# Attention and a two-layer network on one core: the second group's first product as seven half-size products, with a new instruction order

## The chip, the cores and the metric

The kernel runs on one core of a Trainium2 chip. A core has five engines with queues of their own: PE multiplies matrices (weights are loaded by rows called PEld), DVE, ACT and POOL work elementwise, SP issues DMAs here (ACT issues a few at the end). PE writes to PSUM only, POOL does not use PSUM in this kernel. The metric is the device time of one execution in microseconds (us); lower is better.

## The reference, cut to what matters

```
q, k, v: (8 batches, 8 heads, 576 rows, 64)
phi(x) = concat(relu(x) * cos(theta), relu(x) * sin(theta))      theta = pi/2 * row / 576
kv  = phi(k)^T v          z = sum over rows of phi(k)
x   = (phi(q) kv) / (phi(q) z + 1e-6)         -> (4608 tokens, 512)
h   = x @ w_in            (512 x 2048)
g   = max(0.01 h, h)
out = g @ w_out           (2048 x 512)
```

Inputs and output are float32; the kernel's products take float16 and add in float32.

## The kernel before, in words

The tokens are worked in nine groups of 512: groups 0 to 7 are the first 512 rows of each batch, group 8 the last 64 rows of all eight batches. For each group the kernel goes through these steps, whose names are used below (`g` is the group):

- `Lq`, `Lk`, `Lv`, `Lw1`, `Lw2` (for groups 0 and 1 and the weights) and `lq`, `lk`, `lv` (later groups) load; `cw` and `w` cast the weights w_in (w1) and w_out (w2) to float16.
- `rq`, `rk` take the relu, `kt` multiplies k by the angles, `q` prepares phi(q), `v` casts v, `kv` sums phi(k)^T v, `ko` copies it out.
- `qT` transposes phi(q) by a DMA, `n` multiplies it by kv, `N` divides (three DVE instructions), `xT` transposes x by a DMA. In groups 0 and 1 the transposes are made on PE (`qt`, `xt`) and copied out (`qo`, `xo`).
- `f` is the first product (x @ w_in), `F` the second (g @ w_out), `O` takes a result out of PSUM and `D` stores it.

The first product of a group takes 64 matmuls of 512 columns in the plain form (`ffn1`, 16 blocks of 128 outputs by four chunks of the 512 inputs), and eight ACT instructions `e` that apply the leaky relu to two blocks each. In the other form (`ffn1s`) the product is cut in quarters and computed by Strassen's scheme in Winograd's variant: seven products of half the size in place of eight. There are four units `u` in a group, and in each seven products `f{g}.{u}.1` to `.7` of four matmuls of 256 columns. Sums of quarters go in and come out: `W` are sums of w1's quarters (eight in all, made once), `X` four sums of x's quarters for each group. A unit has three of the four PSUM banks `ps_f`, and nine elementwise steps: `b`, `s`, `u` copy a bank (DVE or ACT, as the order says), `y`, `z` add on DVE, `a`, `c`, `e`, `d` apply the leaky relu on ACT. The second product takes the same scheme for all groups but group 0 (`G7 = 1`): sums `T` of w2, sums `S` of g, seven products `F{g}.{n}`, sums `M` and `O`. In the kernel before, the first product takes it from group 2 on (`F7 = 2`).

The order of all instructions is written out in the string ORDER, one token for each step. Each engine runs its own instructions in that order; SP's and ACT's DMAs too. `:D`, `:A`, `:P` after a token name the engine (DVE, ACT, POOL), and `@n` the place in a ring of buffers (of staged loads, of PSUM banks or of outputs) that the step's tile takes. A step waits for its inputs, and for the earlier readers of its place. `i` are idle matmuls at the start. The tokens of different groups are interleaved: while the first and second products of one group run on PE, the elementwise work and the transposes of the next are done.

Where the stage of w1's second block lies in `wext`, `Lk1.0` later takes that room, and the sums `W` of w1 take it after that.

Of the kernel before, what the change touches and what calls it, by code (L numbers as in the profile page):

```python
# [37 lines left out]
xo0.1.0:A f0.1.c f0.2.c f0.3.a f0.1.b f0.3.c N0.1.1 cw.2:P cw.3:P xo0.0.1:D Lw1.5 f0.0.b xt0.1.1@0
f0.0.d f0.2.d f0.3.d f0.0.c Lw1.7 Lw1.8 xo0.1.1:D f0.3.e f0.4.a f0.0.e f0.2.e e0.1 cw.4:D f0.4.d
f0.1.d f0.1.e cw.8:D cw.5:D f0.5.a f0.5.d Lw1.6 Lq1@3 rq1.1:D rq1.0:D cw.7:P e0.0 f0.6.a@0 f0.6.d  # L40
f0.7.a q1.3.0:D q1.1.1:D f0.7.d Lw2.0@2 e0.2 q1.0.0:D q1.2.1:D q1.0.1:D q1.2.0:D w0.0:D Lk1.0 w0.2:D
cw.6:P e0.3 Lw2.1@1 q1.3.1:P f0.12@1 w1.0:P f0.13 rk1.0:D W1.1:D W0.1:D f0.14@0 f0.15 kt1.0.0 e0.6
# [1 line left out]
qt1.2@1 F0.2.2 F0.1.0@1 F0.0.2 qt1.0@0 qo1.2:D qt1.1@1 w1.2:A Lv1.0 Lk1.1 v1.0:P qo1.0:D qo1.1:D
kt1.0.1 F0.0.4 F0.1.2 F0.0.6 F0.3.4 F0.3.6 kv1.0@1 F0.1.4 rk1.1:A kt1.1.0 F0.1.6 Lw2.2@0 Lw2.3.0
w2.0:D ko1.0:A n1.1.0@1 F0.2.4 F0.2.6 kt1.1.1 w2.2:A w3.0:A N1.1.0 F0.2.8 F0.3.8 n1.0.0@0 N1.0.0
F0.0.8 F0.3.10 F0.3.12 Lw2.3.2 w3.2:D F0.0.10 F0.2.10 F0.2.12 xt1.0.0@0 F0.2.14 Lv1.1 v1.1:A kv1.1@1
ko1.1:A lq2@3 rq2.0:P rq2.1:A F0.3.14 T1 q2.0.1:P q2.3.0:P O0.2:D@0 lk2@1 lv2.0@2 F0.0.12 n1.0.1@1
q2.2.1:P F0.0.14 O0.0:A@3 O0.3:D@1 n1.1.1 F0.1.8 F0.1.10 N1.0.1 xt1.1.0@1 xt1.0.1@0 F0.1.12 N1.1.1
# [6 lines left out]
F1.1.1.0 S1.1a S1.1b F1.1.1.1 F1.2.0.1 q3.2.0:D S1.1c F1.1.0.1 S1.2a F1.2.1.1 v3.0:A q3.1.0:A
q3.3.1:P q3.0.1:P q3.2.1:P v3.1:A kv3 M1.1:A S1.2b S1.2c F1.6.0.0@0 F1.6.1.0 F1.6.1.1 q3.3.0:A
q3.1.1:D S1.3c F1.6.0.1 O1.2@2 F1.5.0.0@1 xT2 S1.3a W0.3:D X2.1:D f2.0.1 S1.4b X2.2:D X2.3:D
F1.5.0.1 F1.5.1.0 f2.0.5 q3.0.0:A rq4.0:A ko3:A b2.0:A s2.0:A f2.0.6 M1.6 X2.4:P S1.3b f2.0.2 f2.1.1
D0.2 qT3.1 qT3.0 u2.0:D f2.0.3 F1.7.0.0 f2.0.7 rq4.1:A a2.0 z2.0 e2.0 F1.7.1.0 F1.7.1.1 f2.1.5 y2.0  # L60
b2.1:A S1.4a q4.0.0:A s2.1:A q4.1.0:D lv4.0@2 lv4.1 lk4@3 q4.2.1:P f2.0.4 c2.0 F1.5.1.1 n3.0 f2.1.6
D0.3 D1.2 q4.3.0:P q4.0.1:P D0.0 u2.1:A q4.1.1:A d2.0 f2.1.2 W1.2:P F1.7.0.1 f2.1.3 a2.1 W1.4:P
W1.3:P N3.0 lq5@0 f2.1.7 n3.1 f2.2.1 v4.1:P rk4.0:P M1.7 z2.1 F1.4.1.0 F1.4.0.0 rk4.1:P y2.1 f2.2.5
f2.1.4 e2.1 b2.2:A c2.1 f2.2.2 s2.2:A N3.1 n3.2 f2.2.6 q4.3.1:A d2.1 u2.2:A O1.5@0 v4.0:A f2.2.3
F1.3.1.0 F1.3.1.1 f2.2.7 N3.2 z2.2 n3.3 f2.3.1 F1.4.1.1 F1.4.0.1 F1.3.0.0 N3.3 y2.2 O1.4@1 e2.2
kt4.0.0 kt4.0.1 kt4.1.0 b2.3:A q4.2.0:A F1.3.0.1 f2.3.6 F2.1.0.0@0 a2.2 f2.3.5 u2.3:A c2.2 s2.3:A
f2.3.7 f2.2.4 F2.1.1.0 d2.2 f2.3.2 f2.3.3 y2.3 c2.3 a2.3 xT3 kt4.1.1 S2.1a z2.3 O1.3@2 qT4.0 X3.1:P
X3.2:P f2.3.4 d2.3 e2.3 kv4 f3.0.1 b3.0:A f3.0.5 F2.1.0.1 F2.1.1.1 f3.0.6 X3.3:D S2.1b S2.3b f3.0.2
M2.1:A ko4:A s3.0:D F2.2.0.0 f3.0.3 f3.1.1 n4.0 u3.0:A f3.0.7 F2.2.0.1 F2.2.1.0 F2.2.1.1 a3.0 S2.2a
S2.1c S2.3c S2.2c z3.0 e3.0 F2.6.0.0@1 b3.1:A rq5.1:A F2.6.1.0 f3.1.6 f3.1.2 N4.0 O2.2:D@3 S2.2b  # L70
y3.0 n4.1 u3.1:A lk5@2 rk5.0:P F2.6.1.1 f3.1.5 rq5.0:P q5.0.1:P q5.0.0:A X3.4:P qT4.1 D1.3 lv5.0@1
c3.0 rk5.1:A s3.1:A F2.5.0.0@0 f3.1.7 F2.5.1.0 F2.6.0.1 f3.0.4 N4.1 kt5.0.0 f3.1.3 D1.5 D2.2 lq6@3
q5.1.1:P v5.0:P q5.1.0:P d3.0 a3.1 lv5.1 F2.5.1.1 kt5.0.1 y3.1 z3.1 M2.6 n4.2 f3.2.1 F2.5.0.1 f3.1.4
f3.2.5 S2.3a e3.1 b3.2:A N4.2 kt5.1.0 kt5.1.1 f3.2.6 u3.2:A f3.2.2 F2.7.1.0 qT5.0 D1.4 f3.2.7 c3.1
a3.2 n4.3 F2.7.1.1 s3.2:A N4.3 d3.1 y3.2 f3.3.5 F2.7.0.0 F2.7.0.1 M2.7 f3.2.3 z3.2 O2.5@0 S2.4a
f3.3.1 S2.4b rq6.1:A s3.3:A q5.2.1:A c3.2 e3.2 v5.1:P q5.2.0:D S3.1a f3.2.4 S3.3a F2.4.0.0 b3.3:A
q5.3.1:D f3.3.3 kv5 F2.4.1.0 ko5:A d3.2 xT4 f3.3.6 F2.4.0.1 f3.3.2 n5.0 F2.4.1.1 rq6.0:P q5.3.0:P
u3.3:A f3.3.7 z3.3 X4.1:D S3.2a f4.0.1 F2.3.0.0 F2.3.0.1 y3.3 q6.1.0:P X4.2:P a3.3 F2.3.1.0 f4.0.5
f3.3.4 e3.3 O2.4@3 lk6@2 F2.3.1.1 b4.0:A f4.0.6 f4.0.2 N5.0 n5.1 F3.1.0.0@1 D2.5 s4.0:A c3.3 d3.3
q6.0.1:D q6.0.0:D S3.1b F3.1.1.0 F3.1.1.1 f4.0.3 u4.0:A O2.3@0 X4.3:D S3.2b f4.0.7 lq7@0 a4.0 S3.1c  # L80
f4.1.5 f4.1.1 F3.1.0.1 F3.6.0.0@0 N5.1 z4.0 D2.4 rk6.0:A e4.0 F3.6.1.0 S3.3c S3.2c b4.1:A qT5.1
F3.6.0.1 F3.6.1.1 f4.1.2 rq7.0:P q6.2.0:P q6.2.1:P rq7.1:P q6.3.0:P y4.0 M3.1:D X4.4:D n5.2 f4.1.6
F3.2.1.0 F3.2.1.1 rk6.1:A q6.1.1:A s4.1:A a4.1 u4.1:A c4.0 q6.3.1:A f4.1.3 f4.0.4 f4.1.7 F3.2.0.0
N5.2 M3.6 S3.3b z4.1 y4.1 d4.0 lv6.0@1 n5.3 F3.2.0.1 f4.2.1 F3.7.1.0 F3.7.0.0 F3.7.0.1 f4.2.5
# [1032 lines left out]
```

## Time and profile before

| | us |
|---|---|
| median of 3 runs (lowest, highest) | 277.46 (276.22, 277.86) |
| profiled execution | 278.54 |
| its span, first to last instruction | 276.7 |
| mean granted clock of PE in it | 0.994 |

The page of the profile gives busy time by engine and the chain of work that ended last. Further views are used: busy time of each engine in a stretch of the span (with the number of instructions in brackets, then PE's granted clock, the DMA engines' busy share and GB/s); groups of instructions by line; and the timeline, whose columns are start, duration, engine, line, operation, tile written and tile read, shape and count, and in square brackets the idle time of the engine before it and what ended it. In the chain the columns are start, duration, and the engine and line of the work. PEld is the weight load, SPq and ACTq are an engine's instructions that issue DMAs. A row with a count merges neighbours; instructions on DVE and ACT overlap a little, so that the distance of two starts is less than a duration. L624 is the plain first product, L647 the plain second product, L763 the first product in half-size form, L846 the second in that form, L677 all the elementwise sums of two tensors, L787 the activations of the half-size form, L633 those of the plain form, L420 and L422 copies on ACT and on DVE or POOL.

### The profile page before, as it was taken

What the parts mean: (1) busy time and instruction counts of PE and PEld (TensorE: products, weight loads), DVE (VectorE), ACT (ScalarE), POOL (GpSimd) and SP (SyncE); (2) the same over time, 40 slices, a digit from 0 to 9 for tenths busy, and PEclk for the clock granted to TensorE, in tenths of its full rate; (3) what the DMA queues carried; (4) which work ended last, traced back from release to release, by engine and by line L of the source; (5) the groups of instructions that cost most, each with busy time, mean ns of one, the idle gap of its engine ahead of it and who ended that gap; (6) DMA issues with size and microseconds to landing.
All of it is one profiled execution on the core that took longest, in us unless ns stands there. A gap on an engine that the chain in (4) does not pass through costs nothing.

```text
span 276.7 us, 7179 instructions
## 1 busy us (share of the span) xinstructions
PE 263.6 (95%) x2942; PEld 222.3 (80%) x2942; DVE 222.0 (80%) x433; ACT 173.8 (63%) x278; POOL 81.4 (29%) x86
## 2 busy tenths in 40 slices
PE   8699999999989999997999999999999999999992
PEld 3366555555888999997999899999998999999981
DVE  4673797798989899999997899999688868867652
ACT  6645644898958977785787576665447636475300
POOL 2143130702349436562506440623111004000000
PEclk9999999999999999999999999999999999999997
DMA  6999999999999999999999957095660063110016
GB/s 220 360 357 388 401 406 374 357 195 372 221 196 357 232 233 199 378 207 320 260 221 212 347 124 154 5 207 128 159 152 2 0 121 111 39 39 11 30 25 206
DMA packets 77265, 57.62 MB, mean 208 GB/s; under 512 B 49456, under 2 KB 65840, under 8 KB 76848
## 3 DMA queue, kind: packets, MB, share of 16 engines
q1 hardware_dynamic: 76624, 56.63, 74.7%
q10 hardware_dynamic: 608, 0.52, 0.7%
q8 instruction: 23, 0.38, 0.6%
q14 instruction: 10, 0.08, 0.1%
HBM read 36.70 MB, written 9.44 MB: 167 GB/s over the span
## 4 chain that ended last, share of the span: by engine, by line
PE 68%; DMA 14%; DVE 11%; issue 3%; SPq 1%; ACT 1%; POOL 1%; DVEq 0%; ACTq 0%
PE ps L846 27%; PE ps_f L763 26%; DMA qst<-in_q_dram 6%; PE ps_h L624 5%; DMA xT<-xs 5%; PE ps_o L647 4%; PE ps_kv L444 2%; PE ps_num L544 2%; DMA w1st<-in_moe_w_in_dram 2%; DVE qp L414 2%; DVE ext L677 1%; DMA out_dram<-osb 1%; DVE y L677 1%; DVE g L677 1%; DVE xs L560 1%
## 5 line engine op out<-in xcount | busy, mean ns | idle before, releaser
L787 ACT ACTIVATE g<-ps_f 128x512 f16<-128x512 f32 x84 | 48.9, 599 | 35.0 <-PE ps_f L763 20.2
L846 PEld LDWEIGHTS <-g 128*128 128x128 f16 x640 | 61.7, 98 | 6.5
L846 PE MATMUL ps<-w,g 128*128 128x256 f16 x496 | 65.3, 273 | 0.0
L763 PEld LDWEIGHTS <-w 128*128 128x128 f16 x448 | 48.7, 113 | 4.3 <-issue 3.5
L763 PE MATMUL ps_f<-xT,w 128*128 128x256 f16 x336 | 49.3, 273 | 2.2 <-DMA xT<-xs 2.2
L763 PEld LDWEIGHTS <-wext 128*128 128x128 f16 x336 | 36.7, 114 | 0.6
L846 PE MATMUL ps<-T,ext 128*128 128x256 f16 x240 | 32.6, 273 | 0.0
L624 PE MATMUL ps_h<-xT,w 128*128 128x512 f16 (+1 forms) x144 | 29.2, 356 | 0.2 <-ACT xT L420 0.2
L846 PEld LDWEIGHTS <-ext 128*128 128x128 f16 x256 | 24.8, 98 | 2.6
L763 PE MATMUL ps_f<-X,wext 128*128 128x256 f16 x176 | 26.3, 273 | 0.0
L624 PEld LDWEIGHTS <-w 128*128 128x128 f16 x144 | 15.7, 114 | 10.4
L677 DVE TENSOR_TENSOR ps_f<-ps_f,u 128x512 f32<-128x512 f32 x28 | 19.4, 694 | 4.8 <-PE ps_f L763 3.5
L677 DVE TENSOR_TENSOR y<-ps_f,s 128x512 f32<-128x512 f32 x28 | 19.1, 683 | 3.7 <-PE ps_f L763 3.5
L633 ACT ACTIVATE g<-ps_h 128x1024 f16<-128x1024 f32 x16 | 16.0, 1023 | 7.5 <-PE ps_h L624 7.3
L787 ACT ACTIVATE g<-y 128x512 f16<-128x512 f32 x28 | 17.8, 634 | 3.8 <-DVE y L677 3.8
L560 DVE TENSOR_TENSOR xs<-ps_num,rden 128x512 f16<-128x512 f32 x28 | 19.3, 691 | 1.0
L395 DVE TENSOR_TENSOR kp<-kst,ang 128x1152 f16<-128x1152 f16 x24 | 18.8, 805 | 0.7 <-ACT kst L385 0.7
L420 ACT COPY ps_f<-ps_f 128x512 f32<-128x512 f32 x25 | 14.3, 573 | 5.9 <-PE ps_f L763 5.3
L763 PE MATMUL ps_f<-X,w 128*128 128x256 f16 x112 | 16.9, 273 | 0.7 <-DVE y L677 0.4
L846 PE MATMUL ps<-ext,g 128*128 128x256 f16 x128 | 17.4, 273 | 0.0
L677 DVE TENSOR_TENSOR osb<-ps,ext 128x512 f32<-128x512 f32 x23 | 15.7, 682 | 2.0 <-PE ps L846 2.0
L763 PE MATMUL ps_f<-xT,wext 128*128 128x256 f16 x112 | 16.8, 272 | 0.0
(131 smaller groups left out, 431.9 us busy)
## 6 DMA issues: line engine op xcount, KB each, us to landing
out_dram<-osb SPq DMA_DIRECT2D x32, 256.0 KB, 3.4
qst<-in_q_dram SPq DMA_DIRECT2D x7, 1024.0 KB, 10.6
...
w2st<-in_moe_w_out_dram SPq DMA_DIRECT2D x3, 1024.0 KB, 12.7
...
```

Of the source, the lines that this page charges most:

```text
L395: nc.vector.tensor_tensor(out=st["kp", b][:, lo:hi, :, f * D : (f + 1) * D].rearrange("p c j (x y) -> p (c j) x y", y=2), in0=halved("k", ...
L414: eng.tensor_scalar(out=o, in0=i, scalar1=0.0, scalar2=col, op0=ALU.max, op1=ALU.mult)
L420: nc.scalar.copy(o, i)
L444: nc.tensor.matmul(ps[:, o, (c - lo) * NE : (c - lo + 1) * NE], lhsT=st["kp", b][sl, c, j, :], rhs=vm[sl, c, j, :], start=(j == 0), stop=( ...
L560: nc.vector.tensor_tensor(out=xs, in0=ps[:, :, 0 : 4 * NE].rearrange("p a (b e) -> p a b e", e=NE)[:, :, :, 0:D], in1=rden.rearrange("p (a ...
L624: nc.tensor.matmul(ps[:, m % 2, lo:hi], lhsT=w1[m // 4, c][0][:, w1[m // 4, c][1], m % 4 : 512 : 4], rhs=xT[:, lo // P : hi // P, c, :], s ...
L633: nc.scalar.activation(g_tile(g)[:, 2 * i : 2 * i + 2, :], st["h", g, i], AF.Lrelu)
L647: nc.tensor.matmul(st["ps_o", g, tt], lhsT=st["g", g][:, m, tt * P : (tt + 1) * P], rhs=w2[:, m, :], start=(m == 0), stop=(m == NFT - 1),)
L677: eng.tensor_tensor(out=o, in0=a, in1=b, op=op)
L763: nc.tensor.matmul(ps[:, mi * HT : (mi + 1) * HT], lhsT=a[:, c, 2 * r0 + mi : 512 : 4], rhs=b[:, c], start=(n in (1, 5) and mi == 0 and c ...
L787: nc.scalar.activation(g_tile(g)[:, m : m + 2, r * HT : (r + 1) * HT], {"a": A, "c": y22, "e": E, "d": B_}[e].rearrange("p (m t) -> p m t" ...
L846: nc.tensor.matmul(ps[:, tt], lhsT=a[:, i, tt * P : (tt + 1) * P], rhs=b[:, i], start=(first and i == 0), stop=(i == NPR - 1 and (apart or ...
```

## The change

Three things change.

1. `F7 = 1`: group 1's first product is also computed by `ffn1s`: the steps `f1.0` to `f1.15` and `e1.0` to `e1.7` of the plain form go, and `f1.{u}.{n}`, `X1.1` to `X1.4` and nine elementwise steps for each of four units come. The eight sums `W` are needed for group 1's first product now; before, they were first needed for group 2's.
2. The dummy matmul in front of the first half-size product reads w1 instead of w2. It stands in front of `(g, u, n) == (1, 0, 1)`; before, group 1 did not come to that line, so the matmul was not issued.
3. The whole string ORDER is another one: the order of the steps, the engines that some are given to, and the places in the rings.

By the tokens of the two orders, the engines of the steps that can go to several are (DVE / ACT / POOL):

| steps | before | after |
|---|---|---|
| `q` | 17 / 20 / 27 | 6 / 16 / 42 |
| `X` | 12 / - / 16 | 19 / - / 13 |
| `W` | 5 / - / 3 | 8 / - / 0 |
| `b` | 3 / 25 / - | 3 / 29 / - |
| `s` | 9 / 19 / - | 7 / 25 / - |
| `u` | 10 / 18 / - | 4 / 28 / - |
| `rq` and `rk` | 6 / 17 / 15 | 6 / 14 / 18 |

```diff
-    F7 = 2
+    F7 = 1
...
         if (g, u, n) == (1, 0, 1):
-            nc.tensor.matmul(B_, lhsT=w2[:, 0, 0:P], rhs=w2[:, 0, :], skip_group_check=True)
+            t = w1[0, 0][0]
+            nc.tensor.matmul(B_, lhsT=t[:, 0, 0:P], rhs=t[:, 1, :], skip_group_check=True)
```

From ORDER, the start, the stretch in which group 1's first product begins, and the end:

```diff
-i.10@1 i.13@0 Lq0.0@3 rq0.0:A qt0.1.0@1 i.11@0 Lk0.0@0 Lq0.1 i.14@1 i.7@1 qt0.0.0@0 i.4@1 rq0.1:A
...
-f0.8@1 f0.9 e0.7 f0.10@0 f0.11 q1.1.0:A e0.4 qt1.3@1 qo1.3:A e0.5 F0.2.0 F0.3.0 F0.0.0@0 F0.3.2
...
-xo1.0.1:D xo1.0.0:A q2.2.0:A q2.1.1:A F0.1.14 xo1.1.0:D xt1.1.1@0 q2.1.0:D q2.0.0:D xo1.1.1:A f1.4.0
-f1.0.0@1 f1.1.0 f1.1.2 f1.5.0 f1.0.2 rk2.1:A v2.0:A f1.5.2 rk2.0:P kt2.0.0 kt2.1.1 kt2.0.1 q2.3.1:A
...
-F8.5.1.0 F8.5.1.1 F8.2.0.1 M8.7 F8.4.0.0 O8.5.1@2 F8.5.0.0 S8.4a F8.5.0.1 F8.3.1.0 S8.4b F8.4.1.0
-F8.3.1.1 O8.5.0@0 F8.4.0.1 F8.4.1.1 O8.3.1@1 D8.5.1 O8.2:A@3 D8.2 D7.4 D7.3 F8.3.0.0 D8.3.1 D8.5.0
-F8.3.0.1 O8.4@2 D8.4 O8.3.0@3 D8.3.0
+Lk0.0@2 rk0.0:A Lq0.0@1 Lq0.1 Lv0.0@3 kt0.0.0 rq0.0:A qt0.1.0@1 i.6@1 kt0.0.1 rq0.1:D v0.0:D Lv0.1
...
+rk1.1:D q1.0.0:D W1.1:D W1.2:D w0.0:A w0.2:P Lw2.1@2 Lv1.0 w1.2:P f0.11 w1.0:D F0.0.0@0 e0.5 e0.4
+W1.3:D F0.0.2 F0.2.0 F0.3.0 F0.1.0@1 qt1.3@1 qo1.3:A qt1.2@0 F0.3.2 F0.2.2 qt1.0@1 F0.2.4 F0.0.4
...
+xo1.0.0:D xo1.1.0:D lk3@0 f1.1.1 X1.1:D q2.3.1:A X1.3:P X1.2:D f1.0.1 f1.0.5 F0.1.8 s1.0:A b1.0:D
+f1.0.6 u1.0:A f1.0.2 f1.0.3 f1.0.7 F0.1.10 a1.0 f1.1.5 F0.1.12 F0.1.14 rk3.0:A kt2.0.0 q2.2.0:P
...
+F8.5.1.0 F8.5.1.1 F8.2.0.1 M8.7 F8.4.1.0 O8.5.1@0 F8.4.0.0 F8.4.1.1 S8.4b S8.4a F8.4.0.1 O8.2:A@3
+F8.5.0.0 O8.4@2 F8.5.0.1 O8.5.0@1 D8.5.1 D8.2 D7.5 F8.3.1.0 F8.3.1.1 O8.3.1@0 D8.4 D8.5.0 F8.3.0.0
+F8.3.0.1 D8.3.1 O8.3.0@3 D8.3.0
```

The loads around w2's first block stand in this order in the two strings: `Lw1.6 Lq1@3 Lw2.0@2 Lk1.0 Lw2.1@1 Lv1.0 Lk1.1 Lw2.2@0` before, `Lq1@2 Lw1.6 Lk1.0 Lw2.0@0 Lk1.1 Lw2.1@2 Lv1.0 Lw2.2@0` after. Around group 4's x, SP's tokens are `lv5.1 qT5.0 D1.4 xT4` before and `lv5.1 qT5.0 D2.5 xT4` after.

More of the change, by code (lines that the diff above doesn't have):

```diff
@@ L38 @@
[L38 to L42, printed above, removed]
-f0.8@1 f0.9 e0.7 f0.10@0 f0.11 q1.1.0:A e0.4 qt1.3@1 qo1.3:A e0.5 F0.2.0 F0.3.0 F0.0.0@0 F0.3.2
@@ L44 @@
[L44 to L49, printed above, removed]
@@ L56 @@
[L56 to L61, printed above, removed]
@@ L62 @@
[L62 to L84, printed above, removed]
@@ new lines @@
+N0.1.1 n0.0.1@0 N0.0.1 Lw1.2 cw.2:P cw.3:A xo0.0.0:A f0.0.a@1 xt0.1.0@0 Lw1.4 f0.1.a Lw1.5 xo0.1.0:A
+xt0.1.1@1 f0.4.a f0.2.a@0 xt0.0.1@0 xo0.1.1:D xo0.0.1:D f0.3.a f0.3.c f0.5.a f0.3.d f0.3.e f0.2.d
+f0.0.c f0.2.c cw.4:D f0.2.e f0.1.c f0.0.b f0.1.b f0.0.d e0.1 f0.4.d f0.0.e f0.5.d f0.1.d f0.1.e
+f0.6.a@0 e0.0 Lw1.7 Lw1.8 cw.8:D i.3@1 Lq1@2 Lw1.6 rq1.0:D cw.5:P cw.7:P f0.7.a rq1.1:D f0.7.d
+cw.6:P f0.6.d Lk1.0 f0.12@1 f0.13 e0.2 e0.3 rk1.0:D q1.1.1:D q1.1.0:A e0.6 q1.3.0:A q1.2.1:D kt1.0.0
+f0.14@0 f0.15 Lw2.0@0 q1.2.0:A e0.7 f0.8@1 f0.9 q1.3.1:A kt1.0.1 f0.10@0 W0.1:D Lk1.1 q1.0.1:D
@@ new lines @@
+n4.3 f3.3.1 F2.4.1.1 b3.3:A N4.3 S3.1a v5.0:P f3.3.5 f3.3.6 f3.3.2 S3.3a f3.2.4 s3.3:A f3.3.3
+F2.3.0.0 F2.3.0.1 lv5.1 kt5.1.0 u3.3:A a3.3 kt5.1.1 c3.2 v5.1:A f3.3.7 y3.3 qT5.0 D2.5 O2.4@3 kv5
+xT4 D2.4 ko5:A c3.3 d3.2 qT5.1 D1.4 f3.3.4 F3.1.0.0@1 X4.1:P S3.2a F2.3.1.0 z3.3 X4.2:P q6.2.0:P
+n5.0 d3.3 N5.0 e3.3 q6.1.0:P q6.0.1:P F3.1.1.0 F2.3.1.1 X4.4:P f4.1.1 f4.0.1 F3.1.1.1 b4.0:A O2.3@3
+S3.1c q6.2.1:P q6.1.1:P f4.0.5 F3.1.0.1 n5.1 f4.0.2 S3.2c S3.3c S3.1b f4.0.6 s4.0:A f4.0.3
+F3.6.0.0@0 F3.6.1.0 S3.2b X4.3:D M3.1:A F3.6.0.1 a4.0 u4.0:A z4.0 N5.1 f4.0.7 f4.1.5 F3.6.1.1
```

138 lines of the change are left out of this document (84 added, 54 removed).

## The prediction

> **What bounds the kernel now.** I read the page's busy shares and chain first, then busy time by stage, then the idle times of TensorE (PE).
>
> ```profile
> PE 263.6 (95%) x2942; PEld 222.3 (80%) x2942; DVE 222.0 (80%) x433; ACT 173.8 (63%) x278; POOL 81.4 (29%) x86
> PE 68%; DMA 14%; DVE 11%; issue 3%; SPq 1%; ACT 1%; POOL 1%; DVEq 0%; ACTq 0%
> ```
>
> PE carries two thirds of the chain, DMA (mostly the loads at the start) and DVE the rest. The next view is busy time in four stretches: from the first `f1` step (53.20) to `f2.0.1` (77.48), to `f4.0.1` (126.44), on to 175.28, and to PE's end.
>
> ```profile
> 53.20:77.48 24.28, 23.47 (x294) 15.58 (x293) 20.80 (x40) 21.18 (x25) 5.39 (x6) 1.00 1.05 255
> 77.48:126.44 48.96, 46.97 (x592) 43.69 (x592) 47.04 (x82) 37.88 (x65) 28.92 (x23) 1.00 1.09 260
> 126.44:175.28 48.84, 48.44 (x544) 45.47 (x545) 44.43 (x87) 33.83 (x59) 17.80 (x18) 1.00 0.91 224
> 175.28:271.40 96.12, 96.11 (x1009) 89.36 (x1008) 74.33 (x142) 50.24 (x91) 14.12 (x14) 1.00 0.33 79
> ```
>
> The columns are length, then busy PE, PEld, DVE, ACT, POOL, granted clock (1.00 throughout), DMA share. In the second stretch DVE is busy 47.04 of 48.96 us: there PE and DVE bound the kernel together. After 175.28 PE is alone. PE's only long idle times in these stretches are two:
>
> ```profile
> 77.48 0.60 PE L763 MATMUL ps_f<-xT,w 128*128 128x256 f16 x4 [0.81 <-DMA xT<-xs]
> 126.44 0.60 PE L763 MATMUL ps_f<-xT,w 128*128 128x256 f16 x4 [1.41 <-DMA xT<-xs]
> ```
>
> Both are a group's first matmuls waiting for the transposed x. I count PE's work by the spacing of its starts, which the chain gives:
>
> ```profile
> 59.46 1.25 PE ps_kv L444 x72
> ...
> 62.81 2.59 PE ps_h L624 x12
> ...
> 69.38 0.27 PE ps_num L544 x8
> ...
> 70.83 6.61 DMA xT<-xs
> ...
> 78.95 2.18 PE ps_f L763 x20
> ...
> 120.21 6.19 DMA xT<-xs
> ```
>
> A 512-column matmul takes 2.59/12 = 0.216 us, a 256-column one 2.18/20 = 0.109, a `kv` sum 1.25. Adding these along the order gives PE 23.0 us of work in the first stretch (24.28 long), 45.9 in the second (48.96), 143.2 from there to PE's end at 271.4 (145.0). So 1.3, 3.1 and 1.8 us were lost there, and 11.1 us before 53.2 (53.2 less 42.1 counted), in the loads.
>
> **The change part by part.**
>
> *The product itself.* Removed: 64 matmuls of 512 columns, 64 x 0.216 = 13.8 us. Added: 4 units x 7 products x 4 = 112 of 256 columns, 112 x 0.109 = 12.2, and the one dummy of 512 columns in front, 0.2. PE work **-1.4 us**, all on the path.
>
> A rule speaks against it: the Trainium skill, "TensorE: Matmul & The Clock Gate", Back-to-back issue gap, gives about 131 ns for a sustained 512-column matmul beside 81 ns for 128 columns. By that the 64 would cost 8.4 us and the 112 at least 9.1, a loss of 0.7 or more where the rows give a gain. The trace's 0.216 and 0.109 are strictly in proportion to columns, and the measurement decides.
>
> *What the product brings to the other engines.* Per unit ACT gets four activations and DVE two sums (`y`, `z`), and three copies `b`, `s`, `u` go where the order says: of the 12, 11 to ACT and one to DVE. Eight 128x1024 activations go.
>
> ```profile
> L633 ACT ACTIVATE g<-ps_h 128x1024 f16<-128x1024 f32 x16 | 16.0, 1023 | 7.5 <-PE ps_h L624 7.3
> L787 ACT ACTIVATE g<-ps_f 128x512 f16<-128x512 f32 x84 | 48.9, 599 | 35.0 <-PE ps_f L763 20.2
> ```
> ```profile
> 22.81 2.85 ACT L633 ACTIVATE g<-ps_h 128x1024 f16<-128x1024 f32 x3 [3.62 <-PE ps_h L624]
> 86.09 1.08 ACT L787 ACTIVATE g<-ps_f 128x512 f16<-128x512 f32 x2
> ```
> ```profile
> 78.41 0.42 DVE L677 TENSOR_TENSOR X<-xT,X 128x512 f16<-128x512 f16 x1
> 78.75 0.42 DVE L677 TENSOR_TENSOR xT<-xT 128x512 f16<-128x512 f16 x1
> 87.39 0.69 DVE L677 TENSOR_TENSOR ps_f<-ps_f,u 128x512 f32<-128x512 f32 x1
> 87.99 0.68 DVE L677 TENSOR_TENSOR y<-ps_f,s 128x512 f32<-128x512 f32 x1
> ```
>
> By starts, a large activation takes (2.85 - 1.02)/2 = 0.92, a small one (and a copy) 1.08 - 0.60 = 0.48, a DVE sum on PSUM 0.60, on fp16 quarters 0.34. I counted both orders between the first `f1` step and `f2.0.1`. ACT: 27 x 0.48 - 8 x 0.92, and two `q`, two `rk` fewer, one `rq` more: +3.5 us. DVE: `y`, `z` and one `b` 9 x 0.60, five more X sums 1.7, less three W sums (1.8), two `q` and one S sum: +4.4. Against the row of the stretch that makes DVE 25.2 and ACT 24.7 us, and PE, which gets 24.1 us to do there, is no longer the longest.
>
> From `f2.0.1` to `f4.0.1` the same count gives PE 48.5 (more of the work lies there), DVE +1.1, ACT -1.8. The three W sums that POOL ran there are done on DVE before `f1`, where DVE was idle a third of the time (31.92 of 50 us busy):
>
> ```profile
> sum 50.00, PE 45.70 PEld 26.51 DVE 31.92 ACT 28.41 POOL 12.03; mean PE 1.43 PEld 0.83 DVE 1.00 ACT 0.89 POOL 0.38
> ```
>
> *POOL beside DVE.* The order gives POOL 42 `q` preparations (27 before), DVE 6 (17 before); 13 of the extra ones fall in the `f1` stretch.
>
> ```profile
> L410 POOL TENSOR_SCALAR qp<-qst,sin_t x12: 692/696/1377, 50.1 to 159.7; 128x512 f16<-128x512 f16 x12
> L414 DVE TENSOR_SCALAR qp<-qst,cos_t x6: 342/524/2217, 53.1 to 129.9; 128x512 f16<-128x512 f16 x6
> ```
> ```profile
> 78.91 1.27 POOL L677 TENSOR_TENSOR X<-xT,X 128x512 f16<-128x512 f16 x1 [6.64 <-DVE X L677]
> 83.12 2.57 POOL L677 TENSOR_TENSOR wext<-wext,w 128x1024 f16<-128x1024 f16 x1
> ```
>
> The 2217 ns of a DVE preparation that takes 342 alone lies at 83.62, inside that 2.57 us POOL sum: the two engines slow one another. For a price: DVE's work in the second stretch is 39.9 us by spacing and 47.04 by the row; the first stretch reads 5% above its count with little POOL; the rest, about 5 us on 28.92 us of POOL, is 0.17 us of DVE for each us of POOL. Bounds: 0 and, from the whole excess, 0.25. POOL in the `f1` stretch rises by 13 x 0.70 + two X sums + one relu = 12.5 us and falls by 6.5 in the next (three W sums go): +6 together, +1.0 of DVE. On this the Trainium skill, "GPSIMD Engine Reference", 8. Key points, says that POOL shares its SBUF interfaces with VectorE, with contention against two-input and 2-port instructions; the row agrees.
>
> So over the two stretches DVE has 20.80 + 47.04 + 5.5 + 1.0 = 74.3 us to do, PE 24.1 + 48.5 = 72.6. At 97.5% busy they last 76.2, PE loses 3.6 us where it lost 4.4: **-0.7**. At 100% it would be -2.6; with dearer contention +2.5.
>
> *The two waits on x.* From the last `num` of a group to the next group's first matmul PE needs cover for division and transpose, about 8 us (in the chain the last `num` before group 2 starts at 69.38, and x lands at 70.83 + 6.61 = 77.44). Cover counted in PE work: 6.9 to 7.8 before group 2, 7.4 to 9.6 before 3, 8.1 to 8.5 before 4. The second wait was made longer by the queue:
>
> ```profile
> 115.02 4.47 SPq L488 DMA_TRANSPOSE qpT<-qp  x1
> ...
> 120.21 2.89 SPq L500 DMA_TRANSPOSE xT<-xs  x1
> ```
>
> `xT4` was issued behind a `qT5.0` and a store, and the same two kinds stand in front of it now, but what `qT5.0` needs is older by then. I take both waits as gone; their time is inside the -0.7, since DVE is late next.
>
> *The loads.* The new queue puts `Lk1.0` (0.59 MB) ahead of `Lw2.0`, and five pairs of `F0` ahead of the first `qt1`.
>
> ```profile
> 18.89 3.55 SPq L281 DMA_DIRECT2D w2st<-in_moe_w_out_dram  x1
> ```
> ```profile
> DMA to landing us min/median/max: 12.6/12.7/14.7
> ```
> ```profile
> 20.65 12.49 PE L624 MATMUL ps_h<-xT,w 128*128 128x256 f16 x66
> 32.98 0.61 PE L510 MATMUL ps_qt<-ident,qp 128*128 128x128 f16 x8
> ```
> ```profile
> 30.00:40.00 10.00, 9.50 (x69) 5.45 (x68) 9.76 (x18) 6.53 (x7) 2.96 (x3) 1.00 1.04 410
> 35.67 1.04 ACT L420 CAST w<-w2st 128x1024 f16<-128x1024 f32 x1
> ```
>
> w2's first block lands at 18.89 + 12.6 = 31.5. Behind another 0.59 MB at 0.41 MB/us that is 32.9, and its cast, now on ACT and POOL, 1.05: 34.0, where PE comes to it at 33.0. Against that `k` and `v` come earlier, and PE's own stall of 0.5 us there can be absorbed. I take **+0.6**, bounds -0.4 and +1.1.
>
> *The end.*
>
> ```profile
> 267.75 0.59 ACT L420 COPY osb<-ps 128x512 f32<-128x512 f32 x1 [6.24 <-DVE g L677]
> ...
> 271.76 0.42 DVE L677 TENSOR_TENSOR osb<-ps_f,ext 128x256 f32<-128x256 f32 x1 [0.52 <-DMA out_dram<-osb]
> ...
> 273.30 0.47 SPq L895 DMA_DIRECT2D out_dram<-osb  x1
> ```
>
> The last sum (271.76) waited 0.5 us for the buffer of `O8.2`, whose copy (267.75) stood behind another store on ACT; the last store left 1.1 us after that sum, behind others on SP. Now `O8.2` is ahead of that store, and products 4 and 5 end earlier than product 3. **-0.5**, bounds 0 and -1.1.
>
> *The remaining order, engines and places.* From `f4.0.1` on DVE has 104.8 us by count, 111.2 before, and only 1.8 us of PE is lost: **-0.3**, bounds -1.0 and +1.0.
>
> Sum: -1.4 - 0.7 + 0.6 - 0.5 - 0.3 = **-2.3**. The profiled execution took 278.54 (1.84 around its span of 276.7) and becomes 276.2; the median shown, 277.46, is 1.1 below it and becomes **275.2**.
>
> **The rivals.**
> 1. *DVE packs fully and the loads do not show.* Two stretches at 100% (-2.6 for -0.7) and nothing for the loads (0 for +0.6): 2.5 better, 272.7. For it: DVE may take sums early or late. Against, 98% is the most that ten us of it show:
>
> ```profile
> 110.00:120.00 10.00, 9.72 (x101) 9.14 (x100) 9.84 (x18) 8.58 (x16) 4.61 (x4) 1.00 1.10 316
> ```
> 2. *Slower: POOL's preparations hold DVE up in the `f1` stretch.* If each us of POOL there costs DVE 0.40 us (16 preparations amid S sums and `kt`), 12.5 us cost 5.0, 2.9 more than at 0.17, all on DVE, which is the bound: with the later stretch unchanged, 278.1. It ends above the old time from 0.36 on. For it: 2217 against 342. Against: 0.25 is what a whole stretch showed.
> 3. *The waits are replaced.* The order moves `xT` but cover before groups 2 and 4 grows by only 0.9 and 0.4, and a late division on a full DVE takes it: the two waits (2.2 us) stay, -0.1 in all: 277.3.
> 4. *The change does not shorten anything*, if PE were not what ends the stage: then the 1.4 is lost, 276.6.
>
> **How the numbers follow.** The measurement of this kernel tells about 1% (2.8 us) from no change, so faster means below 274.7 and slower above 280.2. Forecast 0.42 (274.2 to 276.2), rival 1 0.22, rival 2 0.18 (a third of it beyond 280.2), rivals 3 and 4 together 0.18. A quarter of the forecast and nearly all of rival 1 lie below 274.7: faster 0.31; slower 0.09, with something for a new wait of which no row speaks; same 0.60. The range, from rival 1's end to most of rival 2, is 272.6 to 279.0.
>
> **What would show it.** PE: 112 more 256-column `L763` rows, no `L624` beyond group 0, and spacing 0.109. At `f2.0.1` and `f4.0.1` no bracket "<-DMA xT" above 0.5. From `f1` to `f4` DVE near 97%, about 76 us. `F0.0.0` a bracket near 1 us for the w2 cast. At the end, the last store within 0.5 us of the last sum. It is wrong if PE shows new idle time behind `b`, `s`, `u` in group 1, or DVE fp16 rows of 1 us and more beside POOL.

## The result, and the profile after

The changed kernel takes **276.11 us** (median of 19 runs, 274.58 to 277.35) beside 277.32 for the kernel before on the same chip (19 runs); the ratio is 0.995, with a 95% interval of 0.9927 to 0.9973. That is a small gain, half a per cent, and the interval excludes no change. The profiled execution took 276.79 and its span is 275.0 (before 278.54 and 276.7).

In the kernel after, lines 624, 633, 647, 677, 763 and 846 have become L627, L636, L650, L680, L767 and L850; in the kernels of the experiments they differ from these by a line or a few. The busy shares and the chain of its page:

```profile
PE 264.5 (96%) x2991; PEld 227.5 (83%) x2991; DVE 219.6 (80%) x428; ACT 180.7 (66%) x301; POOL 90.5 (33%) x100
PE 74%; DVE 10%; DMA 9%; SPq 2%; ACT 2%; issue 1%; POOL 1%; DVEq 0%; ACTq 0%
```

PE's share of the chain has gone from 68 to 74%, that of DMA from 14 to 9. The busy time by stretch, cut at the first `f1` step (53.40), `f2.0.1` (78.91), `f4.0.1` (127.64), `f6.0.1` (182.55) and the last matmul; below these, the last two cuts of the kernel before (the first two stand in the prediction):

```profile
53.40:78.91 25.51, 25.26 (x358) 22.16 (x358) 24.46 (x45) 23.60 (x39) 15.60 (x15) 1.00 1.11 267
78.91:127.64 48.73, 48.73 (x619) 46.21 (x618) 44.84 (x87) 37.77 (x66) 22.36 (x23) 1.00 0.99 247
53.40:127.64 74.24, 73.99 (x974) 68.37 (x974) 69.30 (x131) 61.37 (x105) 37.97 (x38) 1.00 1.03 254
127.64:182.55 54.91, 53.16 (x650) 49.67 (x649) 45.97 (x88) 35.60 (x62) 28.03 (x30) 1.00 0.86 221
182.55:270.63 88.08, 87.81 (x866) 81.61 (x865) 67.72 (x128) 48.10 (x87) 8.11 (x8) 1.00 0.31 81
```
```profile
126.44:180.24 53.80, 53.40 (x652) 50.23 (x652) 48.81 (x95) 38.30 (x67) 20.82 (x21) 1.00 0.83 205
180.24:270.78 90.54, 90.54 (x894) 84.30 (x893) 69.49 (x134) 45.77 (x82) 11.10 (x11) 1.00 0.33 80
```

From `f1` to `f4` the two kernels take nearly as long (74.24 and 73.24 us), but by my count of matmul spacings the new order has 3.9 us more of PE work in there, and PE is not idle at all in the second of these stretches. The time lost on PE, step by step, is: from its first transposes to `f1` 7.1 us (6.0 in the kernel before), in the `f1` stretch 1.3 (1.3), from `f2` to `f4` 0.2 (3.1), from `f4` to `f6` 2.3 (0.7), after that 1.3 (0.7). So 2.9 us of waits went and 3.3 came. PE's work fell by 1.0 (1.4 of the product, less two idle matmuls more behind the first transposes), and the first transposes come 0.5 later (6.61, before 6.08). By this count PE ends 0.1 us sooner; in the trace it is 0.15. The other 1.5 us lie behind PE's end. The rows that carry this, first PE's:

```profile
31.05 1.89 PE L627 MATMUL ps_h<-xT,w 128*128 128x512 f16 x8 [1.07 <-ACT g L636]
...
33.19 1.89 PE L627 MATMUL ps_h<-xT,w 128*128 128x512 f16 x8 [0.25 <-ACT g L636]
...
34.91 2.32 PE L650 MATMUL ps_o<-w,g 128*128 128x512 f16 x10
...
78.91 1.04 PE L767 MATMUL ps_f<-xT,w 128*128 128x256 f16 x8
...
127.20 1.04 PE L767 MATMUL ps_f<-xT,w 128*128 128x256 f16 x8
...
179.28 0.60 PE L767 MATMUL ps_f<-X,w 128*128 128x256 f16 x4 [1.52 <-DVE y L680]
```

`f2.0.1` at 78.91 and `f4.0.1` inside the last but one row have no bracket now: both waits on x are gone. A new one stands at 179.28 (`f5.3.4`). Its origin is on SP and DVE:

```profile
170.55 1.31 SPq L254 DMA_DIRECT2D qtl<-in_q_dram  x2
171.97 0.57 SPq L908 DMA_DIRECT2D out_dram<-osb  x1
172.64 3.40 SPq L503 DMA_TRANSPOSE xT<-xs  x1
```
```profile
178.20 0.43 DVE L680 TENSOR_TENSOR X<-xT 128x512 f16<-128x512 f16 x1 [2.18 <-DMA xT<-xs]
178.54 0.68 DVE L680 TENSOR_TENSOR y<-ps_f,s 128x512 f32<-128x512 f32 x1
```

The last division of group 6 ended at 168.8, but its transpose `xT6` stood on SP behind the load `lq8.1`, which waited for its ring place until 170.55. `X6.1` waits for x at the head of VectorE's queue, and the finished product that `y5.3` is to add stands behind it. The end:

```profile
269.52 0.42 DVE L680 TENSOR_TENSOR osb<-ps_f,ext 128x256 f32<-128x256 f32 x1 [0.18 <-PE ps_f L850]
270.06 2.18 SPq L899 DMA_DIRECT2D out_dram<-osb  x3
...
271.32 0.42 DVE L680 TENSOR_TENSOR osb<-ps_f,ext 128x256 f32<-128x256 f32 x1 [0.50 <-PE ps_f L850]
```

The last of these three stores is issued by 272.24, half a microsecond after the last sum; before, SP's last store started at 273.30 and ended at 273.77.

### The profile page after: what moved, and what is told of

Its sections match the earlier page's. It is cut to its first block, busy times and chain, and to the rows that moved or that the text cites. A ratio compares the mean times of both kernels' runs of the same rounds, so it can differ in the third digit from the quotient of the medians.

```text
span 275.0 us, 7300 instructions
## 1 busy us (share of the span) xinstructions
PE 264.5 (96%) x2991; PEld 227.5 (83%) x2991; DVE 219.6 (80%) x428; ACT 180.7 (66%) x301; POOL 90.5 (33%) x100
## 4 chain that ended last, share of the span: by engine, by line
PE 74%; DVE 10%; DMA 9%; SPq 2%; ACT 2%; issue 1%; POOL 1%; DVEq 0%; ACTq 0%
PE ps L850 32%; PE ps_f L767 32%; DMA w2st<-in_moe_w_out_dram 4%; DMA ext<-in_moe_w_out_dram 4%; PE ps_idle L298 3%; DVE xs L563 2%; PE ps_num L547 2%; PE ps_kv L447 2%; DVE kp L398 1%; PE ps_f L850 1%; DMA qtl<-in_q_dram 1%; DVE ext L680 1%; DVE y L680 1%; DVE ps_f L680 1%; DVE T L680 1%
## 5 line engine op out<-in xcount | busy, mean ns | idle before, releaser
L791 ACT ACTIVATE g<-ps_f 128x512 f16<-128x512 f32 x96 | 55.7, 601 | 20.8 <-DVE ps_f L680 10.7
L850 PEld LDWEIGHTS <-g 128*128 128x128 f16 x640 | 61.9, 98 | 6.3
L850 PE MATMUL ps<-w,g 128*128 128x256 f16 x496 | 65.1, 273 | 0.0
L767 PEld LDWEIGHTS <-w 128*128 128x128 f16 x512 | 55.5, 113 | 3.9 <-issue 2.3
L767 PE MATMUL ps_f<-xT,w 128*128 128x256 f16 x384 | 55.8, 273 | 0.3 <-DVE xT L425 0.3
L767 PEld LDWEIGHTS <-wext 128*128 128x128 f16 x384 | 41.7, 113 | 1.6 <-ACT ps_f L423 0.4
L850 PE MATMUL ps<-T,ext 128*128 128x256 f16 x240 | 32.4, 273 | 0.2 <-DVE ext L680 0.2
L680 DVE TENSOR_TENSOR ps_f<-ps_f,u 128x512 f32<-128x512 f32 x32 | 22.2, 694 | 9.1 <-PE ps_f L767 6.5
L767 PE MATMUL ps_f<-X,wext 128*128 128x256 f16 x192 | 28.5, 273 | 0.3 <-ACT ps_f L423 0.3
L850 PEld LDWEIGHTS <-ext 128*128 128x128 f16 x256 | 24.7, 98 | 2.9 <-DVE ext L680 0.3
L680 DVE TENSOR_TENSOR y<-ps_f,s 128x512 f32<-128x512 f32 x32 | 22.0, 687 | 6.0 <-PE ps_f L767 2.7
L423 ACT COPY u<-ps_f 128x512 f32<-128x512 f32 x28 | 16.4, 587 | 13.5 <-PE ps_f L767 13.0
L767 PE MATMUL ps_f<-X,w 128*128 128x256 f16 x128 | 19.3, 273 | 1.5 <-DVE y L680 1.5
L413 POOL TENSOR_SCALAR qp<-qst,sin_t 128x512 f16<-128x512 f16 x20 | 16.0, 810 | 10.0 <-ACT qst L388 9.8
L767 PE MATMUL ps_f<-xT,wext 128*128 128x256 f16 x128 | 19.3, 273 | 0.0
L413 POOL TENSOR_SCALAR qp<-qst,cos_t 128x512 f16<-128x512 f16 x18 | 17.7, 987 | 3.4 <-DMA qpT<-qp 3.2
L423 ACT COPY s<-ps_f 128x512 f32<-128x512 f32 x25 | 14.7, 589 | 5.8 <-PE ps_f L767 5.8
L850 PE MATMUL ps<-ext,g 128*128 128x256 f16 x128 | 17.7, 272 | 0.0
```

What stands on the lines that cost most here:

```text
L413: eng.tensor_scalar(out=o, in0=i, scalar1=col, scalar2=1.0, op0=ALU.mult, op1=ALU.mult)
L423: nc.scalar.copy(o, i)
L680: eng.tensor_tensor(out=o, in0=a, in1=b, op=op)
L767: nc.tensor.matmul(ps[:, mi * HT : (mi + 1) * HT], lhsT=a[:, c, 2 * r0 + mi : 512 : 4], rhs=b[:, c], start=(n in (1, 5) and mi == 0 and c ...
L791: nc.scalar.activation(g_tile(g)[:, m : m + 2, r * HT : (r + 1) * HT], {"a": A, "c": y22, "e": E, "d": B_}[e].rearrange("p (m t) -> p m t" ...
L850: nc.tensor.matmul(ps[:, tt], lhsT=a[:, i, tt * P : (tt + 1) * P], rhs=b[:, i], start=(first and i == 0), stop=(i == NPR - 1 and (apart or ...
```

## The experiments

The ratios are to the kernel before on the same chip, with 95% intervals; they need not be the quotient of the two medians. The first four ran together (before there 278.26), then four (277.89) and four (277.93).

**1. The loads.** `Lw2.0` ahead of `Lk1.0` in a first kernel; in a second one, besides, the activations `e0.6` and `e0.7` on ACT ahead of three preparations of group 1's q.

```diff
-... Lk1.0 ... Lw2.0@0 Lk1.1
+... Lw2.0@0 Lk1.0 ... Lk1.1
```

> The changed kernel with one token moved: the load of w2's first block (Lw2.0) stands in front of Lk1.0 again, as in the kernel before. Theory (two covers at one place): the block lands about 1.5 us earlier, but the last matmuls of group 0's first product still wait 1.2 and 0.4 us for the activations e0.6 and e0.7, so the first F0 stays near 34.9 us and the total moves by less than 0.5 us. Rival (the load alone sets the start): the first F0 comes near 33.4 us and the total falls by about 1.5 us.

> As the run before, and on ACT the activations e0.6 and e0.7 stand in front of the three q1 preparations that wait for the q1 load. Theory: both covers are gone, PE's 1.07 us bracket at f0.8 goes, the first F0 comes near 33.4 us, and the first f1 step about 1 us earlier than 53.4 (the later loads may keep some of it); total about 1 us lower than the changed kernel. Rival (the later loads of w2 set the f1 step anyway): first f1 step stays at 53.4 within 0.3, no gain.

Measured: 276.11 us, 0.9913 [0.9878, 0.9948], and 277.03, 0.9948 [0.9918, 0.9977]. Neither can be told from the changed kernel's 0.995. In the first profile `F0.0.0` starts at 33.19 with no wait, 1.7 us ahead of the changed kernel's. But in the kernel of experiment 2, which has the changed kernel's own order of loads, it starts at 33.20, also with none:

```profile
31.55 1.55 POOL L425 CAST w<-w2st 128x1024 f16<-128x1024 f32 x1 [2.99 <-DMA w2st<-in_moe_w_out_dram]
```

```profile
33.38 1.58 POOL L425 CAST w<-w2st 128x1024 f16<-128x1024 f32 x1 [2.97 <-DMA w2st<-in_moe_w_out_dram]
```

In the first row, of that kernel, w2's block had landed at 31.5 and POOL's half of the cast (31.55 + 1.55) was done when PE came; in the second, of the changed kernel, the same cast started at 33.38. So the wait of 1.3 us for `e0.6` and `e0.7` belongs to the execution and not to the order, and the order of these two loads is worth nothing that shows. In the second profile that wait is gone too, but ACT's half of the cast now stands behind the preparations, and `F0.0.0` waits 1.04 us for it and starts at 34.40, not near 33.4.

**2. `X6.1` behind `z5.3`** on VectorE, so that `y5.3` no longer stands behind the wait for x.

> The changed kernel with one DVE token moved: X6.1, which waits for group 6's transposed x, stands behind y5.3 and z5.3 in place of in front of them. Theory (a DVE queue held by one waiting sum): PE's wait of 1.52 us at f5.3.4 goes, PE's end comes 1.3 to 1.7 us earlier, total about 1.5 us lower than the changed kernel (ratio to the kernel before near 0.990). Rival (PE would be held a little later by the late x itself): f6.0.1 waits instead, gain under 0.5 us.

Measured: 276.38, 0.9946 [0.9916, 0.9975]. The wait at `f5.3.4` is gone, and another has its place, not at `f6.0.1` but at the first `num` of group 7:

```profile
179.99 0.43 PE L547 MATMUL ps_num<-kv,qpT 128*128 128x66 f16 x8 [1.41 <-DMA qpT<-qp]
```

**3. Half of a first product left out**, in group 1 and, in another kernel, in group 7.

```diff
-            for c in range(2):
+            for c in range(1 if g == 1 else 2):     # second kernel: g == 7
...
```

> The changed kernel with half of group 1's first product left out: of its two input chunks only the first is multiplied (56 of 112 matmuls of 256 columns go, 6.1 us of PE by spacing); all other work stays. Theory of the prediction (DVE bounds the stretch from f1 to f2.0.1, 24.5 of 25.5 us busy): the stretch shortens by 1 us or less, DVE is busy over 97% of it, and the total falls by 1 to 3 us, what the stretches behind can still take up. Rival (PE bounds the stretch): it shortens by 5 us or more and the total falls by about 6 us.

> The changed kernel with half of group 7's first product left out (the second chunk of every one of its 28 products: 56 rows of 0.109 us, 6.1 us; the output is not the reference's). Theory A (in the late stretches PE alone sets the time, VectorE being 77% busy there): 4.5 to 6.1 us faster than the changed kernel, against nothing for the same cut in group 1. Theory B (the cut is lost everywhere, to sums and transposes which come at their own pace): under 3 us.

Measured: group 1 278.79, 1.0012 [0.9979, 1.0046]; group 7 272.03, 0.9799 [0.9757, 0.9842]. The same 6.1 us of PE work is worth nothing in group 1 and, against the changed kernel, some 4 us in group 7, a little less than the 4.5 expected. Busy time in the stretch where the work is missing, group 1's first, then group 7's (`f7.0.1` to `f8.0.1`) with and without the cut:

```profile
51.85:77.17 25.32, 21.57 (x301) 16.11 (x301) 24.78 (x44) 23.43 (x39) 15.56 (x15) 1.00 1.10 262
```
```profile
203.47:230.80 27.33, 27.33 (x289) 25.27 (x285) 20.71 (x44) 15.78 (x30) 1.16 (x1) 1.00 0.30 69
```
```profile
203.36:225.94 22.58, 21.86 (x235) 19.46 (x232) 19.40 (x42) 15.06 (x29) 1.07 (x1) 1.00 0.39 83
```

In group 1 the stretch is 25.32 long with the cut and 25.5 to 26.5 without (25.51 in the profile above): VectorE is busy for 24.78 of it and ACT for 23.43, and PE is idle for 3.8. In group 7 the stretch shortens by 4.75.

**4. The form alone, in the order of before.** `F7 = 1` and the new dummy in the kernel before, the 28 product steps and their sums put in the places of the 22 old ones, `W0.2`, `W0.4`, `W0.3` on VectorE just ahead of them and `W1.2`, `W1.4`, `W1.3` among them; then the same with these six sums moved back among the second products of group 0.

> The order, engines and ring places of before, with one thing changed: group 1's first product in its half-size form (the 68 steps of it put in the places of the 30 old ones, in the sequence they have in the changed kernel, W0.2, W0.4 and W0.3 on VectorE just ahead of them, W1.2, W1.4 and W1.3 on VectorE after nine of the products). The rest is as before, the tail and the loads too. Theory A (PE sets the end of that stretch): 64 rows of 0.216 us go, 113 of 0.109 us come, 1.3 us faster than before. Theory B (VectorE, with ScalarE behind it, sets the end of that stretch, as the run without half of this product suggests, so less PE work is worth nothing there): the form brings eight 0.69 us sums and six 0.69 to 1.2 us sums to a VectorE which was busy for 20.8 of 24.3 us, and four more copies of 0.57 us and more to ScalarE, so nothing gained to 3 us slower than before; the sums in PE's gaps in that stretch then rise from 1.3 to 3 us or more.

> As the half-size form in before's order, but the six sums of weights (W0.2, W0.3, W0.4, W1.2, W1.3, W1.4) stand among the second products of group 0 on VectorE, where the changed kernel has them, in place of just ahead of and among the first products of group 1. Theory A (the 13.6 us that the form cost in that order came from VectorE's queue: the sums of the product stood behind the sums of weights, and PE, waiting, ran at half its clock afterwards): PE's waits of 3.0 and 1.5 us for y and X1b go, the stretch from f1.1.1 to f2.0.1 falls from 38.0 to 31 us or less, the clock there from 0.87 to 0.95 or more, the whole to 284 us or less. Theory B (the sequence of products itself is what it waits for, each sum being asked for too soon after its product): the stretch stays over 35 us and the whole over 287.

Measured: 290.32, 1.045 [1.0393, 1.0506], and 290.21, 1.0455 [1.0399, 1.0512]. Both theories of the first were far too small. Its stretch from the first `f1` step to `f2.0.1` takes 38.0 us, and the busy time in two pieces of it is:

```profile
67.00:70.30 3.30, 0.33 (x4) 0.17 (x3) 3.22 (x4) 0.60 (x2) 0.25 (x1) 1.00 1.04 373
72.50:77.80 5.30, 5.30 (x32) 3.77 (x32) 2.77 (x6) 4.74 (x8) 0.00 (x0) 0.50 0.50 159
```
```profile
70.28 0.60 PE L766 MATMUL ps_f<-X,w 128*128 128x256 f16 x4 [2.97 <-DVE y L679]
```
```profile
65.53 1.22 DVE L679 TENSOR_TENSOR T<-w,T 128x2048 f16<-128x2048 f16 x1
66.67 1.22 DVE L679 TENSOR_TENSOR w<-w 128x2048 f16<-128x2048 f16 x1
67.81 1.22 DVE L679 TENSOR_TENSOR ext<-w,T 128x2048 f16<-128x2048 f16 x1
68.94 0.69 DVE L679 TENSOR_TENSOR ps_f<-ps_f,u 128x512 f32<-128x512 f32 x1
69.54 0.68 DVE L679 TENSOR_TENSOR y<-ps_f,s 128x512 f32<-128x512 f32 x1
```

Three sums of w1 (62.94 to 64.9) and the sums `T2`, `T3`, `T4` of w2, which nobody needs soon, run on VectorE ahead of `z1.1` and `y1.1`, which PE waits for: 2.97 us. After that PE runs at half its clock for over 5 us. In the old order the three sums of w2 stood side by side and hurt nobody, since the plain product needs no sums; in the changed kernel's order they stand apart. This wait and the clock behind it are some 5.6 of the 13.7 us by which the stretch is longer than before (38.0 for 24.3); other waits, of 0.3 to 1.6 us, for sums of x, activations and divisions, add up to 7.4, and the clock is halved once more, for 3.41 us from 57.41.

The second kernel goes as neither theory said: its stretch takes 33.3 us, 4.7 less, but the sums moved ahead of `f1` cost 3.4 there (22.3 for 18.9 us from `F0.0.0`). The wait for `y1.1` is gone, though `T2` to `T4` stand in the same place, and waits of 1.97 (for an activation) and 1.55 (for `X1.4`) stand among the products, with half the clock behind them. So no single one of these sums is shown to be the cause of the 12 us; the whole sequence does not fit the old order. Moving `T2` to `T4` was not tried.

**5. The old form in the new order.** The plain product of group 1 put back, its steps in the places of the new ones.

> The changed kernel's order, engines and ring places, with group 1's first product put back into its full-size form: the 22 old product steps in the places of the 28 new ones in proportion to their work, an e1 step behind each finished pair, W1.3 and W0.3 (which overwrite a quarter that the full form reads) and group 1's F, S, M and O steps that stood among the products moved just behind the last one. The 8 sums in PSUM, the X1 sums and the 12 copies and further activations of the half-size form are gone. Theory A (PE sets the end of the stretch, the form is worth its PE work): 1.2 to 1.4 us slower than the changed kernel, near 277.5 where before is near 277.9. Theory B (VectorE and ScalarE set it, so the form only pays back its own sums): VectorE loses some 8 us of work in that stretch and ScalarE 4, PE becomes its only bound, and the time stays within 0.5 us of the changed kernel or falls below it.

Measured: 281.71, 1.0154 [1.0106, 1.0202], 5.6 us above the changed kernel, more than either theory said.

```profile
51.70:81.95 30.25, 26.61 (x308) 17.05 (x308) 20.76 (x35) 17.94 (x20) 11.93 (x14) 1.00 0.90 216
```
```profile
62.81 0.75 PE L444 MATMUL ps_kv<-vm,kp 64*128 64x66 f16 x36 [1.48 <-ACT vm L420]
```

PE is busy 26.61 us in the stretch, about as the form should cost (1.3 more than 25.26), but idle for 3.6, behind a cast on ACT, divisions and the angles on VectorE. Some of that is of the experiment's making: `F`, `S`, `M` and `O` steps of group 1 had to go behind the product. Further on, at 183.98, PE waits 1.59 us for a transposed q and then has half its clock for 3.41 us, which is in the 5.6 too.

**6. The tail.** The list from `F8.5.1.0` on exchanged: the new tail behind the old order, and the old tail behind the new one.

> Before, with the list from F8.5.1.0 on (the last 5 us or so) taken from the changed kernel, the stores D7.4 and D7.3 put ahead of it. Theory A (the tail is where the time came from): the last store, which before goes behind three others 2.2 us after the last sum, goes at once, 1.2 to 1.5 us faster than before. Theory B (the tail's gain needs what the new order does ahead of it): within 0.4 us of before.

> The changed kernel with before's list from F8.5.1.0 on, D7.5 put ahead of it. Theory A (the tail is where the time came from): 1.2 to 1.5 us slower than the changed kernel, so the same time as before or up to 0.3 us below it. Theory B: within 0.4 us of the changed kernel, 1 to 1.6 us below before.

Measured: 276.34, 0.9981 [0.9942, 1.0019], and 277.42, 0.996 [0.9922, 0.9997]. The times do not tell the theories apart. The profiles do, for the tail itself: from the start of `F8.3.0.1` to the end of the span it is 5.92 us in the kernel before (276.7 less 270.78) and 5.44 (275.9 less 270.46) in the changed kernel with the old tail; with the new tail 4.71 behind the old order (274.0 less 269.29) and 4.37 in the changed kernel (275.0 less 270.63). So the tail carries 1.1 to 1.2 of the 1.55 us, whatever is ahead of it.

**7. POOL's preparations twice**, for groups 3 to 5.

```diff
+            for _ in range(2 if eng is POOL and g in (3, 4, 5) else 1):
                 phi_half(eng, qp[:, lo:hi, f * D : (f + 1) * D], src[:, lo:hi], col)
```

> The changed kernel with every preparation of q that POOL makes for groups 3, 4 and 5 made twice, some 16 us more of POOL work between 53 and 128 us, the same results. Theory A (the prediction's price: 0.17 us of VectorE time for each us of POOL work): VectorE's busy time in that stretch rises by 2.7 us, from 69.3 to 72, and as it is 93% busy the stretch gets some 1 to 2 us longer. Theory B (POOL's work costs VectorE nothing but where an operation on 16-bit data in SBUF alone lies beside it: the rows of sums that read PSUM are 0.68 to 0.69 us with POOL busy or not): rises by less than 1.5 us, all of it in rows of kp, ext, g and X; the stretch stays within 0.5 us unless a preparation now comes late for its transpose, which shows as a wait of PE's L547 rows for the DMA of qpT.

Measured: 285.27, 1.027 [1.0212, 1.0327]. Groups on VectorE between 53 and 136 us (busy, mean ns of one), the changed kernel first:

```profile
L398 DVE TENSOR_TENSOR kp<-kst,ang 128x1152 f16<-128x1152 f16 x16 | 13.2, 856 | 0.0
L680 DVE TENSOR_TENSOR osb<-ps,ext 128x512 f32<-128x512 f32 x7 | 4.8, 681 | 0.0
L680 DVE TENSOR_TENSOR g<-g 128x512 f16<-128x512 f16 x6 | 3.1, 547 | 0.0
```
```profile
L398 DVE TENSOR_TENSOR kp<-kst,ang 128x1152 f16<-128x1152 f16 x16 | 15.3, 983 | 3.5 <-POOL kst L390 3.5
L681 DVE TENSOR_TENSOR osb<-ps,ext 128x512 f32<-128x512 f32 x7 | 4.8, 682 | 0.0
L681 DVE TENSOR_TENSOR g<-g 128x512 f16<-128x512 f16 x4 | 2.9, 757 | 0.0
```

The rows on 16-bit tiles in SBUF get longer, 856 to 983 and 547 to 757 ns; a sum that reads PSUM stays at 681. That is theory B's picture, but not its price. Between the same steps, `f1` to `f4.0.1` (51.64 to 135.90 here, 53.40 to 127.64 in the changed kernel, whose row stands above), the busy times are:

```profile
sum 84.26, PE 76.84 PEld 69.05 DVE 74.28 ACT 61.51 POOL 55.18; mean PE 25.61 PEld 23.02 DVE 24.76 ACT 20.50 POOL 18.39
```

VectorE has 5.0 us more (74.28 for 69.30) and POOL 17.2 (55.18 for 37.97): 0.29 us for each us, above the prediction's bound of 0.25 and below the 0.36 from which its rival 2 would have ended above the old time. The stretch is 10.0 us longer, and most of that comes by another way. POOL's relu of k is late behind the doubled preparations, `kp` waits 3.5 us for it, and PE waits 4.7 us for `kp`, which neither theory had. It also waits 1.65 us for a transposed q, as theory B said it might, and after these waits has half its clock for 3.4 us.

**8. `xT6` ahead of `lq8.1`** on SP, with the loads of experiment 1.

```diff
-... lq8.1@0 ... D4.2 ... xT6 qT7.0
+... xT6 lq8.1@0 ... D4.2 ... qT7.0
```

> The changed kernel with Lw2.0 ahead of Lk1.0, and with the transpose xT6 ahead of the load lq8.1 on SP (the load waited for its ring place from 164.4 to 170.6 us, and the transpose, whose rows were ready at 168.8, left at 172.6). Theory A: xT6 leaves near 169, X6.1 on VectorE no longer waits 2.2 us for it, y5.3 behind it neither, PE's wait of 1.5 us at f5.3.4 goes, and the time is 1.0 to 1.7 us below that of the kernel with Lw2.0 alone, near 0.987 of before. Theory B (the transpose of q for group 7, next in the same queue, is what PE waits for next, as it did where X6.1 was put behind z5.3): less than 0.5 us.

Measured: 275.35, 0.9911 [0.988, 0.9943]; with the loads alone it was 0.9913, so theory B holds. `xT6` leaves at 169.99, `X6.1` starts at 176.60, and `f5.3.4` has no wait, but the gain is turned into the wait of experiment 2:

```profile
180.99 0.43 PE L547 MATMUL ps_num<-kv,qpT 128*128 128x66 f16 x8 [1.42 <-DMA qpT<-qp]
```

By the median it is the fastest of those that leave no work out, but its interval overlaps that of the changed kernel.

## Why the prediction was right

The prediction of 275.2 us stands beside 276.11, inside its range; the median fell by 1.2 us, half of the 2.3 forecast. Its sum for the profiled execution was -2.3 and -1.75 was measured, but the terms did worse than the sum, and that it came so near is in part luck. At equal PE work the two profiles differ by -1.4 for the product, -2.9 from `f1` to `f4` (forecast -0.7), +1.9 ahead of `f1` (+0.6), +2.2 from `f4` on (-0.3) and -1.5 at the end (-0.5). `f1` itself starts only 0.2 later, but 1.7 us of group 0's second product, which stood ahead of it, now stand behind it.

- **The product, -1.4, "all on the path".** As a count it is right: 112 rows and the dummy for 64, and 2991 matmuls for 2942. As a saving it is not shown: where this product runs VectorE and ACT end it together with PE, and four times as much PE work could go with nothing gained (experiment 3). What was left out is that form and order hang together. As built here, each alone is slower than the kernel before (290.3 and 281.7 for 277.9), and only the pair is faster; as both of these carry waits of their own making, what the form is worth by itself stays open. Rival 4, "PE were not what ends the stage", had this for the `f1` stretch, and its 276.6 is nearer to the median measured than the forecast.
- **`f1` to `f4`, -0.7.** Both waits on x went, as said, and as said VectorE is late next in the `f1` stretch (24.46 of 25.51). But over the two stretches it is busy for 69.3 us of 74.2 (93%), where 74.3 of 76.2 (97.5%) were forecast, and PE lost 1.5 us for 3.6 (4.4 before). The step that failed is VectorE's work, 5 us too much. The kernel before has the first row below among its groups from 53 to 128 us, and the changed kernel none there; I took these preparations off at 0.30 us each, so that 2.9 us more went with them (5 x 0.58). Another 1.0 was put on for POOL's new work, which in this order lies beside more sums on PSUM (12 `y` and 12 `z` in that time, 8 each before), and those stay at 0.68 to 0.69 us beside it. The last 1 us of the 5 was not traced.

```profile
L414 DVE TENSOR_SCALAR qp<-qst,cos_t 128x512 f16<-128x512 f16 x5 | 4.3, 878 | 0.0
```

- **POOL's price, 0.17 us for each us.** Not a constant. In experiment 7 it is 0.29 on the mean of all that lies beside, with the whole rise in rows on 16-bit SBUF tiles and none in PSUM sums. The Trainium skill, "GPSIMD Engine Reference", 8. Key points, has such a limit, contention with instructions in a 2-port mode or with two SBUF inputs; I cited it and then priced all rows alike. Experiment 7 agrees with it: sums of two SBUF tiles went from 547 to 757 ns, sums with a PSUM input stayed at 681 to 682.
- **The loads, +0.6.** Right in sign. PE was done with group 0's first product at 34.91 (32.98 before), 1.9 us later, but not as described: it waited 1.3 us for the activations `e0.6` and `e0.7`, and no bracket for the cast stands at `F0.0.0`. The cast would have held it as long, for POOL's half ended at 34.96. In six other profiles with the same loads this point comes at 33.2 to 33.5, with neither wait, and in four with the loads and start of before at 31.9 to 33.0. On the mean that is 33.3 and 32.4, so some 1 us of it is the order's, and the rest the execution's.
- **The end, -0.5.** Right in kind (the last store within 0.5 us of the last sum), too small in size: 1.5, of which the tail's own order makes 1.1 to 1.2. The bound of -1.1 was short as well; where the other 0.3 to 0.4 comes from was not tried.
- **The rest from `f4`, -0.3.** Wrong in sign up to `f6`: 1.6 us more lost there, by a load at the head of SP's queue, and 0.6 more behind `f6`, whose cause was not sought. That a moved step takes what is queued behind it along was worked out for `xT4` and not for `xT6`.
- **Rival 2** (slower by POOL) named the mechanism that experiment 7 brought about, but its place was wrong: there POOL hurts more through its own queue than through VectorE's rows.
- **The signs.** No `L627` stands beyond group 0, the spacing is 0.109, and PE has no wait of 0.2 us or more behind `b`, `s`, `u` in the `f1` stretch. Fp16 rows of 1 us and more beside POOL, named as a sign of being wrong, are there from `f1` to `f4` (five, up to 1.59 us, apart from the three sums of w2), but the kernel before has seven, up to 2.22: the sign does not tell the two apart.

Why the gain of the tail does not show in the ratios when it is exchanged alone stays open; the intervals of experiment 6 are wider than it.
